# Attention as one row of tiles with values three tiles behind scores, batch preparation in fixed places, and a first MLP layer that starts before the output weights are prepared

## The chip, the cores and the metric

The kernel runs on one core of a Trainium2 chip. The metric is device time in microseconds (us) of one execution, lower is better. An engine is named as the profile names it: PE is TensorE's matmuls and PEld its weight loads, DVE is VectorE, ACT is ScalarE, POOL is GpSimd, and SP is SyncE, whose queue issues nearly every DMA.

## What is computed

Three stages in a chain. Attention over 4 batches, 8 heads, 576 rows of 64, in which only the scores within tau of their row's maximum count; then a gated MLP over the 2304 rows (called the first MLP here); then a mixture of 8 experts whose weights P come from a Sinkhorn iteration. Cut to what matters:

```python
scores = matmul(q, k.T) / sqrt(64)
scores = where(scores >= max(scores) - tau, scores, -1e9)
x = softmax(scores) @ v                      # 2304 x 512, heads side by side
xn = x / rms(x) * rms_g
x = (silu(xn @ w_gate) * (xn @ w_val)) @ w_out       # 512 -> 1536 -> 512
P = sinkhorn(exp(x @ w_gate2), 8 iterations)         # 2304 x 8
out = sum_e P[:, e] * (relu(x @ w1[e]) @ w2[e])      # 512 -> 1024 -> 512
```

## The kernel before

Every matmul is made in float16 from operands that are split into a high and a low part (high*high, high*low, low*high); the split needs a scale, a copy on ACT for the high part and a subtraction for the low part.

**Attention.** A batch has four row groups of 128 rows and a remainder of 64. A tile (`att_tile`, L254) is one head of one row group, or two heads of a remainder: 128 to a batch's 32 plus 4, 144 in all. For each tile TensorE makes scores S from qT, qX and kT into one of two PSUM buffers (L262); DVE takes the row maximum (L271), ACT the exponential (L276), DVE applies the threshold and the sum (L278); ACT and POOL split the result into hl (L283 to L285); a DMA transpose on SP turns it into eT (L287); then, within the same call, TensorE multiplies eT with the values vs into pv (L299). `att_main` (L339) runs 8 tiles of a row group, divides by the sums, and `finish_x` (L309) normalizes the row group and transposes it into xnT, which has two buffers of two row groups each. `att_rem` (L356) does the same for a remainder.

**Preparation of a batch.** `load_batch` (L140) loads raw keys, queries and values into three buffers; `prep_kq` (L179) finds the scales (GpSimd takes a square root by pow, L160), splits the keys chunk by chunk and transposes both halves of the heads into kT (L211); `prep_v` (L218) splits all values at once into vs; `prep_q` (L238) does one row group of queries.

**The first MLP.** `prep_in` (L412) prepares 512 columns of the gate or value weights: four chunks are loaded as 64-bit words, converted to float32 (`to_f32`, L394: ACT L402, DVE L403, L405, L406), squared on POOL (L425), their norms are summed by a matmul (L426), then scaled on ACT (L434), copied to the high part (L435) and subtracted on POOL for the low part (L436). There are three such groups (`prep_group`, L441). `prep_out` (L453) does 12 chunks of the output weights: conversion, absolute maximum on DVE (L459), a scale product (L476), scaling on ACT (L478), split (L479, L480). `mlp_block` (L494) takes two row groups: 12 column slices of the first layer into gv (L501), each through ACT, two DVE steps and a split into tT (L509 to L516); then the second layer for either row group (L529) and the writing of x2d for the last stage.

**What sets the order.** The program is traced in Python order, and the scheduler of the language lays out a fixed instruction stream for every engine: an instruction goes out when its inputs are there by the scheduler's own time model, the lowest priority number first, which is the trace order unless `tc.high_priority()` lowers it. Buffers (`bufs`) limit how far work runs ahead. In the kernel before, the start is traced as keys and queries of batch 0, weight group 0, values of batch 0; the loop over row groups traces attention at high priority, and after the second row group weight groups 1 and 2 and the output weights, then an MLP block after every second row group:

```python
    for i, (b, c) in enumerate(tiles):
        if c == 0 and b > 0:
            state[b] = prep_batch(b, raws.pop(b))
        ...
            with tc.high_priority():
                att_main(i, b, c)
        ...
        if i == 1:
            prep_group(1)
            prep_group(2)
            prep_out()
        if i % 2 == 1 and i > 1:
            mlp_block(i // 2 - 1)
```

So the MLP block of a pair is traced one pair later. The last stage (from L605 on) starts as the attention buffers are given back.

Of the kernel before, what the change touches and what calls it, by code (L numbers as in the profile page):

```python
# [7 lines left out]
F32 = mybir.dt.float32  # L8
F16 = mybir.dt.float16
# [10 lines left out]
def kernel(  # L20
# [43 lines left out]
    def pow2_scale(mx, n, bits, name, least=2.0**-100):  # L64

        s = small([P, n], name + "_s")
        inv = small([P, n], name + "_i")
        V.tensor_scalar(
            inv.bitcast(I32), mx.bitcast(I32), 0x7F800000, None, ALU.bitwise_and
        )  # L70
        V.tensor_scalar(inv, inv, least, None, ALU.max)
# [7 lines left out]
    half = small([P, 1], "half")  # L79
    V.memset(half, 0.5)  # L80
# [59 lines left out]
    def load_batch(b, which="kqv"):  # L140
        raws = []
        for nm, src in (("k", k), ("q", q), ("v", v)):
            if nm not in which:
                continue
            t = pa.tile([P, H, NW, D], F32, tag="raw", name=f"raw_{nm}{b}", bufs=3)
            nc.sync.dma_start(
                out=t[:, :, 0:NCH, :].rearrange("p h c d -> p h (c d)"),
                in_=src[b, :, 0 : NCH * P, :].rearrange("h (p c) d -> p h (c d)", c=NCH),
            )
            for o in (0, 64):  # L150
                nc.sync.dma_start(
                    out=t[o : o + REM, :, NCH, :],
                    in_=src[b, :, NCH * P : S, :].rearrange("h p d -> p h d"),
                )
            raws.append(t)
        return raws
# [22 lines left out]
    def prep_kq(b, raws):  # L179
        kr, qr = raws  # L180
        st = {}
        s_k, i_k = norm_scale(all_max(row_norms(kr, "km"), "kmx"), 1, 10, f"k{b}")
        qm = small([P, NW], "qm", bufs=2)
        for c in range(NW):
# [12 lines left out]
        st.update(wt=wt, bt=bt, c2=c2, qr=qr, s_q=s_q)  # L197

        st["q0"] = prep_q(b, 0, st)
        kT = [  # L200
            pa.tile([P, H // 2, S], F16, tag="kT", name=f"kT{b}_{a}", bufs=3) for a in range(2)
        ]
        for c in range(NW):
            n = P if c < NCH else REM
            ks = pa.tile([P, H, 2, D], F16, tag="ks", name=f"ks{b}_{c}", bufs=2)
            A.activation(ks[:, :, 0, :], kr[:, :, c, :], AF.Copy, scale=s_k[:, 0:1])
            V.scalar_tensor_tensor(
                ks[:, :, 1, :], kr[:, :, c, :], s_k[:, 0:1], ks[:, :, 0, :], ALU.mult, ALU.subtract
            )
            for a in range(2):  # L210
# [4 lines left out]
        st["kT"] = kT  # L215
        return st

    def prep_v(b, st, vr):  # L218
        s_v, i_v = norm_scale(all_max(row_norms(vr, "vm"), "vmx"), 1, 14, f"v{b}")
        vs = pa.tile([P, 2, H, NW, D], F16, tag="vs", name=f"vs{b}")  # L220
        A.activation(vs[:, 0], vr, AF.Copy, scale=s_v[:, 0:1])
        V.scalar_tensor_tensor(
            vs[:, 1].rearrange("p h c d -> p (h c d)"),
            vr.rearrange("p h c d -> p (h c d)"),
# [5 lines left out]
        st["vs"] = vs  # L230
        st["i_v"] = i_v

    def prep_batch(b, raws):
        st = prep_kq(b, raws[0:2])
        prep_v(b, st, raws[2])
        return st

    def prep_q(b, c, st):  # L238
        qs = pa.tile([P, H, 2, D], F16, tag="ks", name=f"qs{b}_{c}", bufs=2)
        qr, s_q = st["qr"], st["s_q"]  # L240
# [9 lines left out]
        return qT, qX  # L250
# [3 lines left out]
    def att_tile(b, c, st, qT, qX, heads, pv, sums, slot):  # L254

        kT, vs = st["kT"], st["vs"]
        sp = psa.tile([P, 2, 512], F32, tag="S", name=f"S{b}_{c}_{heads[0]}", bufs=2)
        rows = P // len(heads)
        for qq, first in ((qT, True), (qX, False)):
            for i, h in enumerate(heads):  # L260
                for j in range(2):
                    T.matmul(  # L262
                        sp[i * rows : (i + 1) * rows, j, 0:HS],
                        lhsT=qq[:, h, 0:rows],
                        rhs=kT[2 * h // H][:, h % (H // 2), j * HS : (j + 1) * HS],
# [4 lines left out]
        mx = pa.tile([P, 1], F32, tag="mx", name=f"mx{b}_{c}_{heads[0]}", bufs=4)  # L270
        V.tensor_reduce(mx, sv, AX.XY, ALU.max)  # L271
        nt = pa.tile([P, 2], F32, tag="nt", name=f"nt{b}_{c}_{heads[0]}", bufs=4)
        A.activation(nt[:, 0:1], mx, AF.Copy, scale=st["wt"][:, c : c + 1])
        e = pa.tile([P, S], F32, tag="e", name=f"e{b}_{c}_{heads[0]}", bufs=3)
# [7 lines left out]
        hl = pa.tile([P, 2 * S], F16, tag="hl", name=f"hl{b}_{c}_{heads[0]}", bufs=3)  # L282
# [3 lines left out]
        eT = pa.tile([P, 2 * S // P, P], F16, tag="eT", name=f"eT{b}_{c}_{heads[0]}", bufs=3)  # L286
        nc.sync.dma_start_transpose(out=eT, in_=hl)  # L287
        for i, h in enumerate(heads):
            o = pv[i * rows : (i + 1) * rows, slot * D : (slot + 1) * D]
            cols = slice(i * rows, (i + 1) * rows)  # L290
            mm = []
            for cc in range(NCH):
                mm.append((eT[:, cc, cols], vs[:, 0, h, cc, :]))
                mm.append((eT[:, cc, cols], vs[:, 1, h, cc, :]))
# [590 lines left out]
```

## Time and profile before

| | |
|---|---|
| time, median of 3 runs | 2223.94 us (2221.84 to 2225.57) |
| the profiled execution's own time | 2225.15 us |
| its span in the profile | 2223.4 us |
| TensorE busy | 2035.1 us, 92% of the span |
| DVE, ACT, POOL busy | 67%, 39%, 25% of the span |

The span runs from the first to the last event in the profile; the execution's own time has a little around it. Busy times are summed over the span, though the stages have different limits: attention and the first MLP fill roughly the first 800 us, the experts the rest. In the rows below, a row of a table by stage gives the stretch, its length, the busy time of each engine with the number of its instructions, the granted share of TensorE's full clock, the busy share of the DMA engines and what they moved in GB/s. TensorE's matmuls are pipelined, so the mean duration of one is longer than the distance from one to the next.

### The profile page before, as it was taken

To read this page: it belongs to the slowest core of one execution; us is meant where nothing else is said; L and a number is where in the kernel's file an instruction comes from. 1 tells how busy PE (TensorE), PEld (TensorE's weight loads), DVE (VectorE), ACT (ScalarE), POOL (GpSimd) and SP (SyncE) were. 2 spreads that over 40 slices of the span, in tenths; PEclk is the share of its full clock that TensorE was granted. 3 is DMA by queue.
4 is the path that set the end of the run, shared out by engine and by line. 5 is a ranking of instruction groups with operands and counts; after the bars stand their busy time and mean duration, and the time that the engine had idled before them with its cause. 6 is when DMAs were issued, how large, how long until landed. Compare 5 with 4: busy or idle time off the path is not lost.

```text
span 2223.4 us, 35280 instructions
## 1 busy us (share of the span) xinstructions
PE 2035.1 (92%) x13872; PEld 1193.9 (54%) x13872; DVE 1496.0 (67%) x2993; ACT 866.5 (39%) x1738; POOL 549.3 (25%) x638
## 2 busy tenths in 40 slices
PE   1337988999899998999999999999999999999999
PEld 0126667666776754555555555555555555555554
DVE  6997667776774267865676766757667666676554
ACT  4778677776773334221221222212212212222211
POOL 4867556564663321000010000000000000000000
PEclk9958999999999999999999999999999999999999
DMA  8976787777776042010010100001001001000001
GB/s 227 223 182 112 139 149 146 152 147 123 125 128 145 17 105 74 5 37 20 20 39 20 38 20 20 20 19 39 19 20 39 19 20 39 3 36 1 1 24 62
DMA packets 321880, 154.10 MB, mean 69 GB/s; under 512 B 278961, under 2 KB 292401, under 8 KB 321713
## 3 DMA queue, kind: packets, MB, share of 16 engines
q1 hardware_dynamic: 321120, 151.82, 30.4%
q8 instruction: 108, 1.77, 0.3%
q14 instruction: 60, 0.48, 0.1%
q0 software_dynamic: 64, 0.00, 0.0%
q10 hardware_dynamic: 528, 0.02, 0.0%
HBM read 68.18 MB, written 12.98 MB: 36 GB/s over the span
## 4 chain that ended last, share of the span: by engine, by line
PE 67%; DMA 2%; DVE 2%; SPq 1%; issue 1%; ACT 1%; POOL 1%; ACTq 0%; DVEq 0%; POOLq 0%
PE y L810 33%; PE h L764 28%; PE gv L501 4%; PE x L529 2%; SPq L666 1%; DMA w2r<-in_moe_w_dram 1%; DMA eT<-hl 1%; PE S L262 0%; DVE w L618 0%; PE pv L299 0%; DMA x2T<-x2d 0%; DMA w1r<-in_moe_w_dram 0%; PE logits L708 0%; POOL tT L516 0%; DMA qT<-qs 0%
## 5 line engine op out<-in xcount | busy, mean ns | idle before, releaser
L764 PE MATMUL h<-x2T,w 128*128 128x384 f16 x4032 | 704.6, 327 | 7.0 <-DMA x2T<-x2d 3.7
L764 PEld LDWEIGHTS <-w 128*128 128x128 f16 x4032 | 394.6, 98 | 297.4 <-issue 11.8
L825 DVE SCALAR_TENSOR_TENSOR acc<-y,coef,acc 128x512 f32<-128x512 f32 x270 | 198.3, 747 | 281.7 <-PE y L810 281.6
L634 POOL TENSOR_TENSOR w1s<-w1r 128x512 f32<-128x512 f32 x16 | 20.3, 1270 | 1063.2 <-DMA w1r<-in_moe_w_dram 1048.3
L810 PE MATMUL y<-w,hD 128*128 128x512 f16 x864 | 220.0, 379 | 0.0
L810 PE MATMUL y<-w,hA 128*128 128x512 f16 x864 | 211.9, 381 | 1.0 <-DVE acc L825 0.8
L810 PE MATMUL y<-w,hC 128*128 128x512 f16 x864 | 211.2, 381 | 0.2 <-ACT acc L821 0.2
L810 PE MATMUL y<-w,hB 128*128 128x512 f16 x864 | 210.4, 380 | 0.0
L284 POOL TENSOR_TENSOR hl<-e,hl 128x512 f16<-128x512 f32 x144 | 173.1, 1202 | 135.8 <-issue 70.5
L752 ACT ACTIVATE hA<-u 128x384 f16<-128x384 f32 x96 | 50.1, 522 | 342.3 <-DVE u L780 322.0
L501 PE MATMUL gv<-xnT,wg 128*128 128x256 f16 x1296 | 167.0, 276 | 11.8 <-DVE u L511 5.9
L752 ACT ACTIVATE hB<-u 128x384 f16<-128x384 f32 x96 | 50.2, 523 | 312.8 <-DVE u L784 311.9
L501 PE MATMUL gv<-xnT,wv 128*128 128x256 f16 x1296 | 167.1, 275 | 0.0
L529 PE MATMUL x<-wo,tT 128*128 128x512 f16 x648 | 144.5, 379 | 0.0
L501 PEld LDWEIGHTS <-wg 128*128 128x128 f16 x1296 | 126.2, 99 | 32.0 <-issue 14.1
L810 PEld LDWEIGHTS <-hB 128*128 128x128 f16 x864 | 84.7, 98 | 102.6 <-issue 1.1
L278 DVE SCALAR_TENSOR_TENSOR e<-S,nt,e 128x576 f32<-128x576 f32 x144 | 116.8, 812 | 32.7 <-ACT e L276 31.5
L299 PE MATMUL pv<-vs,eT 128*128 128x64 f16 x1792 | 82.8, 200 | 59.0 <-DMA eT<-hl 56.2
L299 PEld LDWEIGHTS <-eT 128*128 128x128 f16 (+1 forms) x2240 | 86.2, 104 | 94.0 <-DMA eT<-hl 80.9
L810 PEld LDWEIGHTS <-hD 128*128 128x128 f16 x864 | 84.7, 98 | 95.7 <-issue 0.6
L501 PEld LDWEIGHTS <-wv 128*128 128x128 f16 x1296 | 126.4, 99 | 16.2 <-issue 0.2
L810 PEld LDWEIGHTS <-hC 128*128 128x128 f16 x864 | 84.9, 99 | 92.5 <-issue 1.4
(254 smaller groups left out, 2950.2 us busy)
## 6 DMA issues: line engine op xcount, KB each, us to landing
w1r<-in_moe_w_dram SPq DMA_DIRECT2D x16, 1024.0 KB, 5.0
w2r<-in_moe_w_dram SPq DMA_DIRECT2D x16, 1024.0 KB, 5.5
wgatew<-in_moe_w_gate_dram SPq DMA_DIRECT2D x12, 512.0 KB, 4.8
wvalw<-in_moe_w_val_dram SPq DMA_DIRECT2D x12, 512.0 KB, 4.1
wo<-in_moe_w_out_dram SPq DMA_DIRECT2D x12, 512.0 KB, 4.1
x2d<-xs SPq DMA_DIRECT2D x24, 256.0 KB, 2.5
qX<-qT SPq DMA_DIRECT2D x40, 128.0 KB, 2.6
raw_k<-in_k_dram SPq DMA_DIRECT2D x4, 1024.0 KB, 6.0
```

The source lines that it names most:

```text
L278: V.scalar_tensor_tensor(ev, sv, nt[:, 1:2], ev, ALU.is_ge, ALU.mult, accum_out=sums[:, slot : slot + 1])
L284: G.tensor_tensor(hl[:, S + REM :], e[:, 0 : NCH * P], hl[:, 0 : NCH * P], ALU.subtract)
L299: T.matmul(o, lhsT=a, rhs=r, start=n == 0, stop=n == len(mm) - 1)
L501: T.matmul(gv[:, a, :], lhsT=w[:, l, kk, f * P : (f + 1) * P], rhs=xt[:, r * KD + kk, :], start=n == 0, stop=n == 3 * KD - 1,)
L529: T.matmul(ps, lhsT=tT[f][:, l, o : o + P], rhs=wo[:, f, r, :], start=n == 0, stop=n == 3 * KF - 1,)
L634: G.tensor_tensor(sm[:, 0], a21, a22, ALU.add)
L666: nc.sync.dma_start_transpose(out=xb[:, :, jj * P : (jj + 1) * P], in_=x2d[rows, :])
L752: A.activation(t[:, 0, :], src, AF.Relu)
L764: T.matmul(ps, lhsT=w[:, a, l, kk, f * P : (f + 1) * P], rhs=xb[:, b * 4 + r * 2 + kk, :], start=n == 0, stop=n == 5,)
L810: T.matmul(ps, lhsT=hs[a][f][:, l, jj * P : (jj + 1) * P], rhs=w2[:, r, f, :], start=n == 0, stop=n == 3 * KH - 1,)
L825: V.scalar_tensor_tensor(acc[i], ps, coef[h][:, i : i + 1], acc[i], ALU.mult, ALU.add)
```

## The change

A tile's value matmuls leave `att_tile` for `att_values`: the tile goes into a list `waiting`, and once more than three tiles wait, the first one's values are issued behind the last score matmul of the present tile (`tc.issue_after`). All tiles of all batches form one list, `row`. `prepare` puts each step of a batch's preparation at a fixed place of the row (o counts the 36 tiles of a batch): raw loads, scales, the two halves of keys (`prep_k`) and of values (`prep_v`), the queries. The row is traced with `attention_order`, which gives it priority numbers ahead of what was traced for the MLP; `first` moves on past the three weight groups, so these stay ahead of the later tiles, while the first layer of block 0, the output weights and its second layer come behind the tiles. `mlp_block` is cut into `mlp_in` and `mlp_out`, and for block 0 the output weights are prepared between the two. In the preparation of weights, square roots are taken by a shift of the exponent on DVE in place of pow on POOL, squares move from POOL to ACT, the low part from POOL to DVE with the scale folded into it (and ACT's scale pass goes), the scale of the output weights from ACT to DVE, and their maximum is replaced by a Square on ACT. The raw words of the output weights go through the buffers x2 and x2t.

The diff, cut to its core:

```diff
-    def pow2_scale(mx, n, bits, name, least=2.0**-100):
+    def pow2_scale(mx, n, bits, name, least=2.0**-100, root=False):
...
+        if root:
+            V.tensor_scalar(
+                inv.bitcast(I32), mx.bitcast(I32), 1, 0x7F800000,
+                ALU.logical_shift_right, ALU.bitwise_and,
+            )
+            V.tensor_scalar(inv, inv, 2.0**64, least, ALU.mult, ALU.max)
...
     def norm_scale(sq, n, bits, name):
-        G.tensor_tensor(sq, sq, half.to_broadcast([P, n]), ALU.pow)
-        return pow2_scale(sq, n, bits, name, 2.0**-60)
+        return pow2_scale(sq, n, bits, name, 2.0**-60, True)
...
+    def prep_k(st, a):
+        b, kr, s_k = st["b"], st["raw_k"], st["k"][0]
+        kT = pa.tile([P, H2, S], F16, tag="kT", name=f"kT{b}_{a}", bufs=3)
+        st["kT"].append(kT)
+        for c0 in range(0, NW, 2):
+            m = min(2, NW - c0)
+            ks = pa.tile([P, H, 2, D], F16, tag="ks", name=f"ks{b}_{c0}_{a}", bufs=2)
+            ks = ks.rearrange("p (c h) l d -> p c h l d", c=2)
+            for c in range(c0, c0 + m):
+                r, o = kr[:, a * H2 : (a + 1) * H2, c, :], c - c0
+                A.activation(ks[:, o, :, 0, :], r, AF.Copy, scale=s_k[:, 0:1])
+                V.scalar_tensor_tensor(
+                    ks[:, o, :, 1, :], r, s_k[:, 0:1], ks[:, o, :, 0, :], ALU.mult, ALU.subtract
+                )
+            for c in range(c0, c0 + m):
+                n = P if c < NCH else REM
                 nc.sync.dma_start_transpose(
-                    out=kT[a][:, :, c * P : c * P + n],
-                    in_=ks[0:n, a * H // 2 : (a + 1) * H // 2].rearrange("p h l d -> p (h l d)"),
+                    out=kT[:, :, c * P : c * P + n],
+                    in_=ks[0:n, c - c0].rearrange("p h l d -> p (h l d)"),
...
+    def prep_v(st, a):
+        b, s_v = st["b"], st["s_v"]
+        vs = pa.tile([P, 2, H2, NW, D], F16, tag="vs", name=f"vs{b}_{a}", bufs=2)
+        st["vs"].append(vs)
+        r = st["raw_v"][:, a * H2 : (a + 1) * H2]
+        A.activation(vs[:, 0], r, AF.Copy, scale=s_v[:, 0:1])
...
+    waiting = []
+    LAG = 3
...
+        waiting.append((st, heads, slot, group, eT))
+        if len(waiting) > LAG:
+            with tc.issue_after(last.ins):
+                att_values(*waiting.pop(0))
+    def att_values(st, heads, slot, group, eT):
+        if slot == 0:
+            group["pv"] = psa.tile([P, H * D], F32, tag="pv", name=f"pv{group['n']}", bufs=1)
+        rows = P // len(heads)
...
-            G.tensor_tensor(sq, raw[:, kk], raw[:, kk], ALU.mult)
+            A.activation(sq, raw[:, kk], AF.Square)
...
-        G.tensor_tensor(n2, n2, half, ALU.pow)
-        s, inv = pow2_scale(n2, 1, 9, f"{name}{gi}", 2.0**-60)
+        s, inv = norm_scale(n2, 1, 9, f"{name}{gi}")
         gs = small([P, KD], f"{name}gs{gi}")
         V.tensor_scalar(gs, g_sb, s[:, 0:1], None, ALU.mult)
         for kk in range(KD):
-            A.activation(raw[:, kk], raw[:, kk], AF.Copy, scale=gs[:, kk : kk + 1])
-            A.activation(w[:, 0, kk, cols], raw[:, kk], AF.Copy)
-            G.tensor_tensor(w[:, 1, kk, cols], raw[:, kk], w[:, 0, kk, cols], ALU.subtract)
+            sk, hi = gs[:, kk : kk + 1], w[:, 0, kk, cols]
+            A.activation(hi, raw[:, kk], AF.Copy, scale=sk)
+            V.scalar_tensor_tensor(w[:, 1, kk, cols], raw[:, kk], sk, hi, ALU.mult, ALU.subtract)
...
+            sq = to_f32(wo32[:, f], wd, f"wol{f}").bitcast(BF16)[:, 0:DM]
+            A.activation(sq, wo32[:, f], AF.Square, accum_out=om[:, f : f + 1])
...
-            A.activation(r, wo32[:, f], AF.Copy, scale=sf[:, 0:1])
+            r = rr[:, f % 2 * 2 : f % 2 * 2 + 2].rearrange("p o d -> p (o d)")
+            V.tensor_scalar(r, wo32[:, f], sf[:, f // n : f // n + 1], None, ALU.mult)
...
+    def attention_order():
+        return tc.high_priority(offset=tc.cur_priority - first)
...
+    SLOTS = len(row) // B
+    def prepare(b, o):
+        st = states[b]
+        if o < NCH * H and o % H == 1:
+            prep_q(st, o // H + 1)
+        if b > 0 and o in (LAG - 3, LAG - 1):
+            prep_v(st, (o - LAG + 3) // 2)
+        if b + 1 == B:
+            return
+        nx = states[b + 1]
+        early = b > 0
+        if o == (4 if early else 20):
+            nx["raw_k"] = load_raw("k", k, b + 1)
+            nx["raw_v"] = load_raw("v", v, b + 1)
+        if o == (10 if early else 23):
+            prep_k_scale(nx)
+        if o == (12 if early else 24):
+            prep_v_scale(nx)
+        if o == (18 if early else 26):
+            prep_k(nx, 0)
+        if o == 25:
+            nx["raw_q"] = load_raw("q", q, b + 1)
+        if o == 28:
+            prep_q_scales(nx)
+        if o == 32:
+            prep_q(nx, 0)
+        if o == 34:
+            prep_k(nx, 1)
...
+    for t in range(len(row) + LAG):
+        before = tc.cur_priority
+        with attention_order():
+            if t < len(row):
+                b, c, heads, n, g = row[t]
+                if n == 0:
+                    g["sums"] = pa.tile([P, H], F32, tag="sums", name=f"sums{g['n']}", bufs=2)
+                att_tile(states[b], c, heads, n, g)
+                prepare(b, t % SLOTS)
+            else:
+                att_values(*waiting.pop(0))
+            done = list(ended)
+            ended.clear()
+            for g in done:
+                (end_main if g["c"] < NCH else end_rem)(g)
+        first += tc.cur_priority - before
+        for g in done:
+            i = g["i"]
+            if i == 1:
+                for gi in range(NG):
+                    prep_group(gi)
+                first = tc.cur_priority
+                tT = mlp_in(0)
+                prep_out()
+                mlp_out(0, tT)
+            elif i is not None and i % 2 == 1 and i < len(tiles) - 1:
+                mlp_out(i // 2, mlp_in(i // 2))
```

## Rows read from the trace of the kernel before

**Rows 1.** Table by stage, all engines: busy us (x instructions), granted clock, DMA.

```profile
12.00:182.00 170.00, 54.17 (x386) 27.90 (x387) 161.50 (x317) 119.89 (x240) 119.07 (x108) 0.79 0.80 199
75.00:182.00 107.00, 40.77 (x353) 24.05 (x353) 104.48 (x205) 76.36 (x159) 80.19 (x76) 0.66 0.76 176
182.00:256.00 74.00, 68.75 (x739) 51.54 (x739) 48.03 (x108) 54.78 (x122) 41.97 (x55) 0.98 0.77 129
256.00:667.00 411.00, 374.06 (x4141) 285.26 (x4141) 287.22 (x682) 307.02 (x701) 259.45 (x349) 0.99 0.75 139
```

**Rows 2.** Waits of PE, 0 to 182 us: total us, times, longest.

```profile
PE pv L299 <- DMA eT<-hl: 32.4, 13, 4.8
PE S L262 <- DVE e L278: 29.3, 9, 6.9
```

**Rows 3.** Waits of PE, 182 to 667 us, same columns.

```profile
PE pv L299 <- DMA eT<-hl: 23.8, 29, 3.1
PE gv L501 <- DVE u L511: 5.9, 5, 2.2
PE pvr L299 <- DMA eT<-hl: 4.5, 4, 1.8
```

**Rows 4.** DMA issues: queue, count, median us to landing.

```profile
eT<-hl SPq DMA_TRANSPOSE x144, 3.4
```

**Rows 5.** Timeline of PE, six pieces: start us, us, instruction, count, idle before.

```profile
182.17 2.72 PE L501 MATMUL gv<-xnT,wg 128*128 128x256 f16 x12 [3.52 <-DMA xnT<-xn]
...
640.24 0.57 PE L299 MATMUL pv<-vs,eT 128*128 128x64 f16 x14
...
641.14 0.57 PE L299 MATMUL pv<-vs,eT 128*128 128x64 f16 x14
...
644.66 1.47 PE L501 MATMUL gv<-xnT,wg 128*128 128x256 f16 x12
...
645.97 1.04 PE L501 MATMUL gv<-xnT,wv 128*128 128x256 f16 x8
...
677.38 15.70 PE L529 MATMUL x<-wo,tT 128*128 128x512 f16 x72
```

**Rows 6.** Lines 0 to 182 us, by form: busy us, mean ns, idle before.

```profile
L262 PE MATMUL S<-kT,qT 128*128 128x288 f16 x46 | 15.2, 428 | 42.8 <-DVE e L278 29.3 <-DMA kT<-ks 10.8 <-DVE wval_i L68 2.3
...
L299 PE MATMUL pv<-vs,eT 128*128 128x64 f16 x266 | 17.1, 236 | 34.0 <-DMA eT<-hl 32.4 <-DVE vs L222 1.5
...
L459 DVE TENSOR_REDUCE om<-wo 128x1 f32<-128x512 f32 x12 | 8.1, 672 | 0.0
```

**Rows 7.** Stage 0 to 182 us of lines 403, 405, 406, 436: busy us.

```profile
0.00:182.00 182.00, 25.38 (x36) 0.80 0.80 200
...
0.00:182.00 182.00, 36.51 (x36) 0.80 0.80 200
...
0.00:182.00 182.00, 30.43 (x36) 0.80 0.80 200
...
0.00:182.00 182.00, 35.19 (x24) 0.80 0.80 200
```

**Rows 8.** Lines 403 and 405, 0 to 182 us: ns min/median/max, first and last start.

```profile
L403 DVE TENSOR_SCALAR wgatel<-wgatew x12: 410/446/1374, 16.0 to 87.0; 128x512 int32<-128x512 int32 x12
...
L405 DVE SCALAR_TENSOR_TENSOR wgatel<-wo,wgatel x12: 678/688/1637, 17.4 to 90.2; 128x512 int32<-128x512 int32 x12
```

**Rows 9.** Lines over the whole span: busy us, mean ns, idle before.

```profile
L278 DVE SCALAR_TENSOR_TENSOR e<-S,nt,e 128x576 f32<-128x576 f32 x144 | 116.8, 812 | 32.7 <-ACT e L276 31.5 <-POOL wo L480 0.6
...
L271 DVE TENSOR_REDUCE mx<-S 128x1 f32<-128x576 f32 x144 | 106.7, 751 | 36.6 <-PE S L262 36.1
...
L510 DVE SCALAR_TENSOR_TENSOR u<-u,gv 128x256 f32<-128x256 f32 x108 | 44.9, 417 | 85.3 <-ACT u L509 84.6
...
L222 DVE SCALAR_TENSOR_TENSOR vs<-raw_v,v_s,vs 128x2560 f16<-128x2560 f32 x4 | 12.8, 3202 | 2.2 <-ACT vs L221 2.2
```

**Rows 10.** Stage 95 to 182 us, PE's matmuls of tile S alone.

```profile
95.00:182.00 87.00, 18.46 (x68) 0.59 0.75 168
```

More of the change, by code (lines that the diff above doesn't have):

```diff
@@ L137, with load_raw @@
     psa = psa_cm.__enter__()
[L140 to L145, printed above, removed]
+    H2 = H // 2
+    def load_raw(nm, src, b):
+        t = pa.tile([P, H, NW, D], F32, tag="raw", name=f"raw_{nm}{b}", bufs=3)
+        nc.sync.dma_start(
+            out=t[:, :, 0:NCH, :].rearrange("p h c d -> p h (c d)"),
+            in_=src[b, :, 0 : NCH * P, :].rearrange("h (p c) d -> p h (c d)", c=NCH),
+        )
+        for o in (0, 64):
             nc.sync.dma_start(
-                out=t[:, :, 0:NCH, :].rearrange("p h c d -> p h (c d)"),
-                in_=src[b, :, 0 : NCH * P, :].rearrange("h (p c) d -> p h (c d)", c=NCH),
-            )
[L150 to L156, printed above, removed]
+                out=t[o : o + REM, :, NCH, :],
+                in_=src[b, :, NCH * P : S, :].rearrange("h p d -> p h d"),
+            )
+        return t
     def norm_scale(sq, n, bits, name):
-        G.tensor_tensor(sq, sq, half.to_broadcast([P, n]), ALU.pow)
-        return pow2_scale(sq, n, bits, name, 2.0**-60)
+        return pow2_scale(sq, n, bits, name, 2.0**-60, True)
     def row_norms(r, name):
@@ L196, in prep_kq @@
         V.tensor_scalar(wt, i_q, i_k[:, 0:1], nz8[:, 0:1], ALU.mult, ALU.mult)
[L197 to L210, printed above, removed]
+        st.update(wt=wt, bt=bt, c2=c2, s_q=s_q)
@@ L354, in att_main, with end_rem @@
         finish_x(i, x, st["i_v"][:, 0:1])
-    def att_rem(b):
-        st = state[b]
-        qT, qX = prep_q(b, NCH, st)
-        pv = psa.tile([P, H * D], F32, tag="pv", name=f"pvr{b}", bufs=1)
-        sums = pa.tile([P, H], F32, tag="sums", name=f"sumsr{b}", bufs=2)
-        for i in range(H // 2):
-            att_tile(b, NCH, st, qT, qX, [2 * i, 2 * i + 1], pv, sums, i)
-        rs = recip_sums(sums[:, 0 : H // 2], H // 2, f"rsumr{b}")
+    def end_rem(group):
+        i, st, pv = group["i"], group["st"], group["pv"]
+        b = st["b"]
+        rs = recip_sums(group["sums"][:, 0:H2], H2, f"rsumr{b}")
         if b % 2 == 0:
@@ L543, in mlp_block @@
             if pool is None:
-                x = pw.tile([P, 2, HD], F32, tag=f"x2{a}", name=f"x2f{i}")
+                if a == 0:
+                    x4 = pw.tile([P, 4, HD], F32, tag="x2", name=f"x2f{j}")
+                x = x4[:, 2 * a : 2 * a + 2]
             else:
@@ L551, in mlp_block @@
         if pool is None:
-            tt = pw.tile([P, 3, HD], F32, tag="x2t", name=f"x2t{j}")
+            tt = pw.tile([P, 4, HD], F32, tag="x2t", name=f"x2t{j}")
         else:
@@ new lines @@
+    first = tc.cur_priority
+    def attention_order():
+        return tc.high_priority(offset=tc.cur_priority - first)
+    row = []
+    for b in range(B):
+        for c in range(NW):
+            if c < NCH:
+                heads = [[h] for h in range(H)]
+            else:
+                heads = [[2 * h, 2 * h + 1] for h in range(H2)]
+            i = tiles.index((b, c)) if c < NCH else tiles.index((b, None)) if b % 2 else None
+            g = dict(st=states[b], c=c, i=i, n=f"{b}_{c}", last=len(heads) - 1)
+            row += [(b, c, hd, n, g) for n, hd in enumerate(heads)]
```

197 lines of the change are left out of this document (93 added, 104 removed).

## The prediction

> **What bounds the kernel now.** I read the table by stage first [rows 1]. From 12 to 182 us VectorE is busy 161.5 of 170 us (104.5 of 107 from 75 us on), while TensorE works in snatches, most of them at the lower of its two clocks (0.66 of full speed granted from 75 us on). From 182 us TensorE leads: 68.8 of 74, then 374 of 411 us. So the start is VectorE's and the rest TensorE's, and the time to win is TensorE's idle time.
>
> What it waits for is the second view [rows 2, 3]. Before 182 us: the transposed weights eT (32.4 us, in front of value matmuls) and the threshold step on VectorE that frees the score buffers (29.3). From 182 to 667 us eT again: 23.8 and 4.5 of (74 - 68.8) + (411 - 374) = 42 us. TensorE takes its instructions in order, so 14 value matmuls whose eT is 3.4 us in the DMA [rows 4] hold up the scores and MLP matmuls behind them.
>
> The timeline gives dates and prices [rows 5]. The first matmul of the first MLP starts at 182.2 us. At full clock 12 gate matmuls take 1.31 us from start to start, so a block's first layer costs 24 x 1.31 = 31.4 us; its second layer takes 15.7; and from one tile's values to the next tile's, with four score matmuls between, it is 0.90 us, the price of a tile.
>
> **TensorE's idle time at the start, before.** By 182 us it has done 46/2 = 23 tiles of scores and 266/14 = 19 of values [rows 6], 19 us, and 24 norm matmuls of 512 columns like the second layer's 15.7/72 = 0.22 us, 5 us. So 158 us are lost, and 74 - 68.8 = 5 more by 256 us, when block 0 is through both layers: 163.
>
> **The change at the start.** It lets the first layer begin as soon as two rows are there, and it reorders, adds to and lightens VectorE's work. That work is what has to be added up, since VectorE was full. By 182 us it has done 22 tiles and all weight chunks in 161.5 us [rows 1].
> - Gone: the 12 maxima of the output weights, 8.1 us [rows 6]. The Squares that replace them and GpSimd's squares go to ScalarE, where as many scale passes leave: no change, it is busy 120 of 170 us [rows 1].
> - New: 24 subtractions from GpSimd (35.2 us there) [rows 7]. Nearest are the other 512-wide instructions with two SBUF inputs, 0.68 us at best and 36.5/36 = 1.01 on average [rows 7, 8]; I take 0.9, as GpSimd gets emptier: 21.6 us (16 to 25). The output weights' scale, 12 times, comes over from ScalarE: as a 512-wide tensor_scalar 0.41 to 0.7, taken as 0.5: 6. The pow steps go from GpSimd to a shift in an instruction that was there: nothing.
> - Cheaper: the conversions of the 36 chunks. They took 25.4 + 36.5 + 30.4 = 92.3 us [rows 7]; at their minima of 0.41, 0.68 and, taken as its like, 0.68 [rows 8] they would take 63.7. These 28.6 us are lost beside GpSimd, busy 119 of 170 us [rows 1]. It loses the 35.2 us and 24 squares of the same shape, say 70 us, so six tenths come back: 17 (0 to 28.6).
> - Newly wanted by the same date: block 0's 24 elementwise steps of 0.417 us (10) [rows 9], a third of block 1's (3.3; four tT buffers let four of its twelve slices in before the second layer frees more), and the next batch's keys and values, which now rank ahead of the MLP (values 3.2 us [rows 9], the keys' ten smaller pieces about 6: 9; that halves double the instruction count costs 0.1 us a piece and is in it).
> Sum: 161.5 - 8.1 + 21.6 + 6 - 17 + 22.3 = 186 us, and 0.812 + 0.751 = 1.6 us for each tile past 22 [rows 9].
>
> How many tiles run before the output weights are ready no row shows. Tiles now outrank that preparation, up to a cap: xnT has two buffers, so the row stops when block 2 (to tile 52) wants a third, at about 54. The least is 24, with block 1 half done. Nearest is the rate of now: from 95 to 182 us 68/4 = 17 score tiles [rows 10], 5.1 us each; from some 50 us on that makes 30 to 33, and I take 30. Then VectorE needs 199 us: 57 by 75 us, as now, the other 142 at 0.976, date 75 + 145 = 220 us. TensorE has by then 30 x 0.9 + 31.4 + 10.5 + 5 = 74 us of work behind it and 146 idle: **17 us won** of 163. With 24 tiles: 211 us, 69 of work, 142 idle, 21 won. With 54: 260, 96, 164, nothing. The first gate matmul moves much further, to about 100 us (scores from 30 us, 16 tiles of 3 to 4 us, some 10 us to xnT); most of that lead is spent waiting for VectorE.
>
> Queues: SP keeps its 144 transposes for eT, its loads and the keys' transposes, at other dates. A raw load for the next batch stands in the row, and would hold up the eT transposes behind it if it had to wait for its buffer; it is asked for after the buffer's last reader, so I cost it at nothing. What covers it is the lag of three tiles; without that each batch would stall for part of a load.
>
> **From there to 667 us.** With values three tiles behind, eT has about three tiles' time, 12 us, for a 3.4 us transfer, so of the 28.3 us of waits 24 go; 4 stay where a group ends and the one pv buffer has to be read out. Late next is the chain of the scores (two buffers, freed by the threshold step). Bounds: 28 (nothing late next) and 5 (nearly all renamed). What follows attention changes no instruction: 0.
>
> **Sum.** The profiled execution took 2225.15 us (span 2223.4), 1.2 above the median of the runs, 2223.94. 2225.15 - 17 - 24 = 2184; against the median 2183.
>
> At one place the Trainium skill bears on the ledger. The rows show one conversion at 0.41 or at 1.37 us, the two-input one at 0.68 or 1.64 [rows 8]. GPSIMD Engine Reference, section Key points, says that GpSimd shares its SBUF interfaces with VectorE, and that they collide in VectorE's two-port mode and in instructions with two SBUF inputs. The spread agrees. The moved subtraction has two SBUF inputs, which speaks against moving it; emptying GpSimd speaks for it. By the rule alone all of the 28.6 us could come back instead of 17, as in the first rival.
>
> **Rivals.**
> - *Weights first, no collisions (faster, 2152).* Tiles only fill gaps, so 24 stand at the date (21 won), conversions run at their minima (11.6 us of VectorE, 12 won), all 28 us for eT go, and 10 of the other 14 us of waits from 182 to 667 us: 71 us. For it: VectorE is the only full engine and its conversions are stretched. Against: tiles outrank weights, and GpSimd keeps its part of every tile.
> - *The wait changes its name (2204).* ScalarE has 307 us of work in the 411 [rows 1]; packed into less, and in bursts whenever xnT comes free, its MLP steps come late, and TensorE waits for those in place of eT: 5 of 28 won, 15 at the start. Against: today TensorE waits for such steps 5.9 us [rows 3].
> - *The output weights starve (slower, 2244).* Their preparation ranks below every tile that the cap allows. With 54 tiles ahead, no relief in the conversions (+17) and the subtractions at 1.01 (+3), VectorE needs 186 + 51 + 20 = 257 us, the date is 280, and 96 us of work leave 184 idle, 21 lost; a stretch that tight leaves 5 of the eT gain at best, and loads that wait in the row cost a few us more: 19 lost. It comes out slower once the date passes 96 + 163 + 5 = 264 us, or 283 with the eT gain whole.
> That the change would not do what it says is hardly a rival: the lag is written into TensorE's queue.
>
> **How the numbers follow.** 0.46 for the forecast, 0.27 for weights first, 0.13 for the renamed wait, 0.14 for starving. About 4.5 us (0.2%) is what a measurement can tell from no change. Faster: 0.45 + 0.27 + 0.10 = 0.82; same: 0.01 + 0.02 + 0.02 = 0.05; slower: 0.01 + 0.12 = 0.13. The range runs from 2130, weights first with the bounds of its tile count and of the moved instructions, to 2222, which leaves out most of the starving case.
>
> **What would show it.** In the changed kernel's table by stage VectorE is 95% busy until about 220 us; the first gate matmul comes near 100 us, the second layer near 220, with about 30 tiles before it; waits of values for eT after that are under 6 us; conversions lie between their minima and today's means. It would be wrong if VectorE had holes before 200 us, the second layer came before 190 or after 260 us, or a new wait of over 15 us stood in the middle stretch.

## The result, and the profile after

The changed kernel took 2196.59 us (median of 4 runs, 2195.02 to 2199.54), the kernel before 2222.89 us beside it (4 runs, 2216.88 to 2225.57): a ratio of 0.989, 95% interval 0.9875 to 0.9904, so 1.1% or some 26 us faster. The forecast was 2183 in a range of 2130 to 2222: the sign and the range held, and of the 41 us forecast 26 came. The profiled execution took 2195.02 us (span 2193.2).

The table by stage of the changed kernel answers to [rows 1], with the same columns: stretch, length, busy time of TensorE, weight loads, VectorE, ScalarE and GpSimd, granted clock, DMA share and GB/s.

```profile
12.00:182.00 170.00, 75.55 (x634) 46.86 (x635) 154.40 (x340) 137.11 (x291) 57.68 (x64) 0.82 0.88 215
75.00:182.00 107.00, 58.45 (x587) 41.22 (x586) 98.53 (x208) 87.00 (x192) 49.87 (x56) 0.71 0.85 185
182.00:256.00 74.00, 61.08 (x637) 44.10 (x635) 59.08 (x143) 56.33 (x127) 45.12 (x53) 0.95 0.67 136
256.00:667.00 411.00, 386.91 (x4174) 292.50 (x4171) 286.93 (x679) 299.80 (x693) 246.41 (x337) 0.98 0.73 136
```

Read the TensorE column against [rows 1]. By 182 us it has been busy 21.4 us longer (75.55 against 54.17), from 182 to 256 us 7.7 less, from 256 to 667 us 12.9 more: 13.7 of the gain was there at 256 us, and 12.9 came later. GpSimd's time at the start has halved, from 119.07 to 57.68 us. VectorE is still nearly full (154.40 of 170).

The waits of TensorE, 0 to 182 us, answer to [rows 2]; those from 182 to 667 us, in the second fence, to [rows 3] (total us, times, longest).

```profile
PE pv L330 <- DMA eT<-hl: 27.6, 10, 4.7
PE wgaten L457 <- ACT wgateq L456: 24.5, 10, 9.4
PE S L282 <- DVE e L298: 19.1, 7, 6.9
```

```profile
PE pv L330 <- DMA eT<-hl: 19.6, 19, 3.8
PE S L282 <- DVE e L298: 5.2, 5, 1.9
PE S L282 <- DVE xm L571: 4.9, 1, 4.9
PE gv L530 <- DVE u L540: 2.7, 4, 1.5
PE pv L330 <- DVE xrem L395: 2.2, 1, 2.2
```

The surprise is the first line of the second fence: values still wait 19.6 us for eT, where [rows 3] had 23.8 and 4.5. A lag of three tiles was to have removed nearly all of it.

The conversions of the 36 weight chunks in 0 to 182 us (lines 433, 435 and 436, which are 403, 405 and 406 of [rows 7]), and in the fourth row the 24 subtractions that came over from GpSimd (line 466; the second figure, in us, is VectorE's):

```profile
0.00:182.00 182.00, 16.81 (x36) 0.83 0.88 215
...
0.00:182.00 182.00, 26.58 (x36) 0.83 0.88 215
...
0.00:182.00 182.00, 26.75 (x36) 0.83 0.88 215
...
0.00:182.00 182.00, 21.26 (x24) 0.83 0.88 215
```

The three steps take 70.1 us where they took 92.3, and the subtractions cost 21.3.

Two dates on the timeline of TensorE (compare [rows 5]: the first MLP matmul was at 182.17):

```profile
156.66 2.74 PE L530 MATMUL gv<-xnT,wg 128*128 128x256 f16 x12 [1.36 <-DMA xnT<-xn]
...
210.38 1.89 PE L561 MATMUL x<-wo,tT 128*128 128x512 f16 x8
```

The second layer of block 0 starts at 210.4 us (236.4 before). That date is a good yardstick: up to it TensorE has executed much the same in either kernel (954 matmuls in the changed one: scores of all 36 tiles of batch 0, the values of all but the last few, one first layer). The stretch from 12 us to that date, first of the kernel before, then of the changed one:

```profile
12.00:236.40 224.40, 104.09 (x1011) 70.01 (x1012) 199.68 (x405) 165.26 (x341) 157.41 (x158) 0.83 0.79 181
```

```profile
12.00:210.40 198.40, 101.64 (x954) 68.66 (x955) 182.40 (x410) 161.18 (x351) 79.51 (x88) 0.85 0.83 198
```

The date moved by 26 us: VectorE had 17.3 us less to do before it (199.68 to 182.40) and was idle 8.7 us less (24.7 to 16.0). Half of that was given back at once. From 220 to 240 us TensorE is busy only 13.3 us, because batch 1's scores and block 1's rows are not ready yet: in the second fence of waits, the 4.9 us are one wait of scores there. So a date that is 26 us earlier is worth 13.7 us of TensorE's time at 256 us.

### The profile page after: what moved, and what is told of

Its sections match the earlier page's. It is cut to its first block, busy times and chain, and to the rows that moved or that the text cites. A ratio compares the mean times of both kernels' runs of the same rounds, so it can differ in the third digit from the quotient of the medians.

```text
span 2193.2 us, 35334 instructions
## 1 busy us (share of the span) xinstructions
PE 2032.0 (93%) x13872; PEld 1194.7 (54%) x13872; DVE 1490.2 (68%) x3026; ACT 870.9 (40%) x1774; POOL 471.0 (21%) x572
## 4 chain that ended last, share of the span: by engine, by line
PE 70%; DVE 2%; DMA 1%; SPq 1%; POOL 0%; issue 0%; ACT 0%; DVEq 0%; ACTq 0%
PE y L906 33%; PE h L860 28%; PE gv L530 5%; PE x L561 2%; PE pv L330 1%; DMA w1r<-in_moe_w_dram 1%; SPq L762 0%; PE S L282 0%; DMA x2T<-x2d 0%; DVE w L714 0%; DMA w2r<-in_moe_w_dram 0%; DMA eT<-hl 0%; PE logits L804 0%; DVE w1m L725 0%; POOL xh L601 0%
## 5 line engine op out<-in xcount | busy, mean ns | idle before, releaser
L304 POOL TENSOR_TENSOR hl<-e,hl 128x512 f16<-128x512 f32 x144 | 172.8, 1200 | 228.2 <-ACT hl L303 146.2
L330 PE MATMUL pv<-vs,eT 128*128 128x64 f16 (+1 forms) x2240 | 103.1, 201 | 50.3 <-DMA eT<-hl 47.3
L330 PEld LDWEIGHTS <-eT 128*128 128x128 f16 (+1 forms) x2240 | 91.0, 106 | 79.1 <-DMA eT<-hl 62.1
```

The lines of the kernel that those rows point to most:

```text
L304: G.tensor_tensor(hl[:, S + REM :], e[:, 0 : NCH * P], hl[:, 0 : NCH * P], ALU.subtract)
L330: T.matmul(o, lhsT=a, rhs=r, start=n == 0, stop=n == len(mm) - 1)
```

## The experiments

Any edit makes the kernel's planner (the scheduler of the language) lay out every queue anew, and two small edits (the scale on ScalarE, the late loads below) came out 2 to 4 us off the changed kernel without a clear cause. With intervals of 0.0009 to 0.0017 on either side, a difference of under some 5 us between two variants is not read as an effect here. "Lost" below is the ratio less 0.989, times 2222.

| kernel | ratio to before (95%) | median us | lost us | second layer at | TensorE busy 12 to 256 | idle 256 to 667 |
|---|---|---|---|---|---|---|
| before | 1 | 2222.9 | 24 | 236.4 | 122.9 | 36.9 |
| changed | 0.9890 (0.9875 to 0.9904) | 2196.6 | 0 | 210.4 | 136.6 | 24.1 |
| VectorE step doubled | 1.0023 (1.0014 to 1.0032) | 2226.9 | 30 | 233.8 | 120.6 | 35.0 |
| GpSimd loaded | 1.0039 (1.0025 to 1.0054) | 2230.8 | 33 | 228.2 | 125.1 | 37.9 |
| two conversion steps | 0.9868 (0.9854 to 0.9882) | 2191.9 | -5 | 205.1 | 145.2 | 26.0 |
| and output squares on VectorE | 0.9905 (0.9888 to 0.9922) | 2199.2 | 3 | 198.6 | 148.5 | 30.6 |
| old division of weights | 0.9997 (0.9988 to 1.0006) | 2221.1 | 24 | 226.4 | 124.1 | 32.2 |
| before with new division | 0.9972 (0.9961 to 0.9982) | 2215.6 | 18 | 225.7 | 131.2 | 37.2 |
| output weights first | 0.9907 (0.9894 to 0.9921) | 2202.2 | 4 | 217.5 | 135.0 | 28.4 |
| scale on ScalarE | 0.9907 (0.9891 to 0.9923) | 2200.2 | 4 | 214.4 | 137.2 | 25.8 |
| planner's own lag | 0.9925 (0.9912 to 0.9939) | 2205.9 | 8 | 210.2 | 138.0 | 32.0 |
| lag of four | 0.9885 (0.9872 to 0.9898) | 2196.5 | -1 | 217.9 | 137.1 | 25.6 |
| preparation at the end | 0.9935 (0.9921 to 0.9949) | 2207.1 | 10 | 213.7 | 136.5 | 33.6 |
| late loads | 0.9901 (0.9885 to 0.9916) | 2200.7 | 2 | 211.4 | 137.7 | 25.0 |

The last two columns come from the table by stage of each profile. In most rows, what is lost there against the changed kernel adds up to about what the run lost; the loaded GpSimd (25 of 33) and the output squares are the exceptions.

The two columns cut every kernel at the same dates. A kernel that is late as a whole shows only a part of that before 256 us, and the rest as idle time behind it. So a second measure is needed: how late a kernel is at equal work. Every kernel here runs the same 13872 matmuls. The changed one has started 250,000 columns (of moving data, summed over its matmuls) at 262 us; against that, and against the end of its profiled span, the others are late by (us, minus for early):

| kernel | at 250,000 columns | at the end |
|---|---|---|
| before | 15.7 | 30.2 |
| VectorE step doubled | 27.7 | 35.1 |
| GpSimd loaded | 26.6 | 35.8 |
| two conversion steps | -12.3 | -6.8 |
| and output squares | -14.0 | 3.7 |
| old division | 17.6 | 23.3 |
| planner's own lag | -1.4 | 11.0 |
| preparation at the end | 2.7 | 12.2 |

(One profiled execution each; the ends lie up to some 6 us from what the medians give.) Most of what the doubled step and the loaded GpSimd cost is there at the start, though the stage table splits it about in half; the last two lose nearly all of theirs behind it.

### Is the start VectorE's?

**VectorE step doubled.**

```diff
         V.scalar_tensor_tensor(
             di, word[:, :, 1], -(2**31), lw, ALU.bitwise_and, ALU.bitwise_or
         )
+        V.scalar_tensor_tensor(
+            di, word[:, :, 1], -(2**31), lw, ALU.bitwise_and, ALU.bitwise_or
+        )
```

> The changed kernel with the third conversion step of each of the 36 weight blocks done twice (it repeats itself without changing anything): 36 more operations on VectorE, 26.8 us by the durations of the changed kernel, all before the output weights are ready. Theory 'VectorE's queue sets the end of the start': the second layer goes from 210 to 233 us or later and the kernel to 2214 to 2224 us (18 to 27 us more). Rival 'the weights' transfers or ScalarE set it': 2205 us or less.

Measured: 2226.9 us, 30 lost (a little above the theory's 18 to 27), second layer at 233.8. The added steps took 29.0 us by its profile:

```profile
12.00:240.00 228.00, 28.99 (x36) 0.80 0.74 176
```

They are paid in full, so VectorE's queue sets the date; transfers and ScalarE did not hide any of it.

**GpSimd loaded.**

```diff
-            to_f32(raw[:, kk], wd, f"{name}l{gi}_{kk}")
+            lw = to_f32(raw[:, kk], wd, f"{name}l{gi}_{kk}").bitcast(BF16)[:, 0:DM]
+            for _ in range(2):
+                G.tensor_tensor(lw, raw[:, kk], raw[:, kk], ALU.mult)
```

> The changed kernel with 48 more products on GpSimd, two behind the conversion of each of the 24 gate and value blocks; nothing reads them, and nothing else changes. GpSimd's busy time in 12 to 182 us goes from 57.7 to about 110, as under the old division. Theory 'VectorE's operations grow where GpSimd works beside them, and VectorE sets the end of the start': the 36 conversions go from 70 back to about 90 us and the kernel to 2212 to 2224 us (0.8 to 1.3 times the growth). Rival 'the old division cost by its chain over GpSimd, not by collisions': 2193 to 2204 us.

Measured: 2230.8 us, 33 lost, more than either theory's range. Nothing on VectorE was added, yet its conversions take 87.2 us, as the stretch from 12 to 240 us of lines 433, 435 and 436 shows (in the fourth row GpSimd's 48 products, line 456):

```profile
12.00:240.00 228.00, 21.97 (x36) 0.84 0.77 177
...
12.00:240.00 228.00, 33.90 (x36) 0.84 0.77 177
...
12.00:240.00 228.00, 31.37 (x36) 0.84 0.77 177
...
12.00:240.00 228.00, 58.11 (x48) 0.84 0.77 177
```

Against 70.1 in the changed kernel that is 17 us for 58 us of GpSimd's work; the 24 subtractions grew by 2.5 more (23.7). Single durations show how, ns min/median/max; first the changed kernel, then this one with GpSimd's products under it:

```profile
L435 DVE SCALAR_TENSOR_TENSOR wgatel<-wo,wgatel x12: 673/680/1637, 20.5 to 95.0; 128x512 int32<-128x512 int32 x12
```

```profile
L435 DVE SCALAR_TENSOR_TENSOR wgatel<-wo,wgatel x12: 680/1214/1637, 20.5 to 126.9; 128x512 int32<-128x512 int32 x12
...
L456 POOL TENSOR_TENSOR wgatel<-wo x24: 1034/1156/2168, 22.3 to 133.2; 128x512 bf16<-128x512 f32 x24
```

The minimum and the maximum stand where they stood; the median went from 680 to 1214 ns. An instruction meets a GpSimd operation or it doesn't, and one that does takes up to 0.96 us more, nearly the length of such an operation (1.03 at least).

The Trainium skill, SBUF — State Buffer, section "SBUF: two separate sides", says that the port pair shared by VectorE and GpSimd is an exclusive lock held for a whole instruction, and that the other engine blocks until then. These rows agree.

That GpSimd's work at the start costs VectorE time, and VectorE's time costs the run, is shown. VectorE's own work up to the second layer grew by 21 us (203.37, from 182.40). The other 12 of the 33 us are not accounted for. The products also stand in GpSimd's queue among what it does for the tiles and the first MLP, and this run does not tell that from the collisions.

**Two conversion steps.**

```diff
-        V.tensor_scalar(lw, word[:, :, 0], 29, None, ALU.logical_shift_right)
         di = dst.bitcast(I32)
-        V.scalar_tensor_tensor(lw, di, 3, lw, ALU.logical_shift_left, ALU.bitwise_or)
+        V.tensor_scalar(lw, di, 3, 4, ALU.logical_shift_left, ALU.bitwise_or)
```

> The changed kernel with a conversion of two steps on VectorE in place of three: the shift and the merge of the low word are left out, so that the weights carry 21 bits and not 24. VectorE loses 36 operations, 43.4 us to some 17 us of two of the three, 26 us in all. Theory 'VectorE sets the end of the start, in both directions': second layer near 190 us, 2170 to 2180 us. Rival 'ScalarE (137 of 170 us) or the transfers take over as soon as VectorE is relieved': 2186 to 2197 us.

Measured: 2191.9 us, 5 less than the changed kernel by the point values, with intervals that overlap. It is the one variant that may beat both kernels. Its stretch from 12 us to its second layer:

```profile
12.00:205.10 193.10, 98.96 (x953) 66.93 (x953) 164.32 (x389) 165.79 (x363) 75.06 (x94) 0.89 0.85 206
```

VectorE does 18 us less than in the changed kernel, and the date moves 5; TensorE's busy time up to 256 us rises by 8.6. VectorE's idle time rose from 16 to 29 us, ScalarE is now the fuller of the two (165.8 us). So what VectorE gets on top is paid in full, and of what it is spared only a part comes back: the second theory held.

**And output squares on VectorE.** On top of two steps, to relieve ScalarE.

```diff
-            A.activation(sq, wo32[:, f], AF.Square, accum_out=om[:, f : f + 1])
+            V.scalar_tensor_tensor(
+                sq, wo32[:, f], 1.0, wo32[:, f], ALU.mult, ALU.mult, accum_out=om[:, f : f + 1]
+            )
```

> The kernel with two conversion steps (weights of 21 bits, no low word), and the 12 squares of the output weights, 8.6 us of ScalarE, taken by VectorE instead (about 9 us there). With two steps VectorE was down to 172.9 of 208 us and the gain only 5 us. Theory 'ScalarE (169.5 of 208 us) was the next limit of the start': second layer before 202 us in place of 205.1, 2183 to 2188 us. Rival 'no engine is the limit any more, but the chain of the tiles through all of them': 2189 to 2196 us.

Measured: 2199.2 us, outside both ranges. The date did what ScalarE's theory asked (198.6 us), and TensorE's busy time up to 256 us is the highest of all. That is not more work, though: 1367 matmuls where two steps alone have 1383 (the columns agree within 0.5%), at a clock of 0.87 for 0.90. The run is slower all the same: in the middle stretch TensorE idles 30.6 us, and the granted clock from 256 to 400 us is 0.94 (0.98 in the changed kernel, 0.95 with two steps alone).

```profile
256.00:400.00 144.00, 126.76 (x1339) 91.66 (x1340) 99.85 (x245) 110.78 (x252) 80.46 (x110) 0.94 0.81 151
```

The start was lost early in this stretch: from 286 to 340 us TensorE ran 439 matmuls at 0.84, where two steps alone ran 491 at 0.94. An earlier start is not kept by itself. What let it slip there stays open.

### Which part of the change earned it?

**Old division of weights**, in the changed kernel; the output weights' Squares on ScalarE stay.

```diff
-            A.activation(sq, raw[:, kk], AF.Square)
+            G.tensor_tensor(sq, raw[:, kk], raw[:, kk], ALU.mult)
...
-            A.activation(hi, raw[:, kk], AF.Copy, scale=sk)
-            V.scalar_tensor_tensor(w[:, 1, kk, cols], raw[:, kk], sk, hi, ALU.mult, ALU.subtract)
+            A.activation(raw[:, kk], raw[:, kk], AF.Copy, scale=sk)
+            A.activation(hi, raw[:, kk], AF.Copy)
+            G.tensor_tensor(w[:, 1, kk, cols], raw[:, kk], hi, ALU.subtract)
...
-            V.tensor_scalar(r, wo32[:, f], sf[:, f // n : f // n + 1], None, ALU.mult)
+            A.activation(r, wo32[:, f], AF.Copy, scale=sf[:, f // n : f // n + 1])
```

> The changed kernel with the old division of the weight preparation: squares and low halves of the gate and value weights back on GpSimd, a scale pass of ScalarE ahead of the copy, the scale of the output weights back on ScalarE. VectorE loses 24 subtractions (21.3 us) and 12 scales, GpSimd gets 48 operations. Theory 'lighter GpSimd at the start earned it' (17 us of conversions): 2208 to 2216 us, conversions back to about 92 us in the first 182 us. Rival 'order earned it': 2192 to 2200 us, the conversions' loss paid by the 21 us of subtractions that VectorE is spared.

Measured: 2221.1 us: with the old division the rest of the change gains nothing. The conversions took 91.4 us, to within a microsecond those of before (0 to 240 us, lines 433, 435, 436):

```profile
0.00:240.00 240.00, 26.36 (x36) 0.85 0.74 182
...
0.00:240.00 240.00, 31.40 (x36) 0.85 0.74 182
...
0.00:240.00 240.00, 33.67 (x36) 0.85 0.74 182
```

VectorE's own total up to the second layer is only 7 us above the changed kernel's (189.5 us), since it is spared the subtractions; the rest of the 16 us by which that date is later is idle time of VectorE (25 us for 16). So the division gains in two ways, by fewer collisions and by fewer holes.

**Before with new division.** The same three edits the other way round, in the kernel before, which keeps its maxima and its 12 small scale instructions on VectorE.

> The kernel before with nothing changed but the division of the weight preparation (squares on ScalarE, low halves and the output scale on VectorE, no scale pass on ScalarE). Theory 'lighter GpSimd at the start earned it': 2203 to 2212 us. Rival 'order earned it' (tiles in one row, batch preparation in fixed places, first layer ahead of the output weights): 2218 to 2228 us, as the kernel before.

Measured: 2215.6 us, 5 to 6 us faster than before: between the two theories. Conversions 69.5 us, second layer 10.7 us earlier, 8.3 us more TensorE work by 256 us; nothing in the middle stretch (37.2 us idle). So neither the division nor the order brings the 26 us alone: 6, nothing, and 24 to 26 together. The two runs do not cut the change cleanly, since the maxima and the small scales stay with the order in both.

**Output weights first.**

```diff
-                tT = mlp_in(0)
                 prep_out()
-                mlp_out(0, tT)
+                mlp_out(0, mlp_in(0))
```

> The changed kernel with the output weights prepared ahead of the first MLP layer of block 0 (one line moved). If the early first layer fills TensorE's idle time in the stretch bound by VectorE: 6 to 10 us slower than the changed kernel (2202 to 2207 us), first gate product after 180 us. If the stretch is bound by VectorE whatever the order: 2194 to 2199 us, with the second layer earlier than 210 us by what the first one is later.

Measured: 2202.2 us, 4 lost, at the edge of what can be told and at the foot of the first theory's range. The first MLP matmul did not move (158.4 us for 156.7), against the first theory: it waits for its rows, not for its place. The second layer came 7 us later, against the second.

**Scale on ScalarE.**

```diff
-            V.tensor_scalar(r, wo32[:, f], sf[:, f // n : f // n + 1], None, ALU.mult)
+            A.activation(r, wo32[:, f], AF.Copy, scale=sf[:, f // n : f // n + 1])
```

> The changed kernel with the 12 scales of the output weights (8.6 us on VectorE) back on ScalarE as in the kernel before. Theory 'VectorE's queue sets the end of the start': second layer 5 to 9 us earlier than 210, 2188 to 2192 us. Rival 'the last blocks of the output weights hang on their chain, not on VectorE's queue, and ScalarE is the longer one in it': 2196 to 2202 us.

Measured: 2200.2 us, within what can't be told from the changed kernel; second layer at 214.4, 4 us later although VectorE has less to do: as the second theory had it. Just ahead of the second layer ScalarE is then the full engine (20.00 of 20 us from 200 to 220).

### What is the lag worth?

**Planner's own lag.** The values stand where the planner puts them.

```diff
-        waiting.append((st, heads, slot, group, eT))
-        if len(waiting) > LAG:
-            with tc.issue_after(last.ins):
-                att_values(*waiting.pop(0))
+        att_values(st, heads, slot, group, eT)
...
+        if o in (34, 35):
+            prep_v(nx, o - 34)
```

> The changed kernel, but the value products of a tile stand where the program's own scheduler puts them; everything else of the change stays. In the instruction order of TensorE the kernel before already had 3 or 4 scores tiles ahead of most values (103 of 144; 1 to 7 in all), the changed kernel 3 or 4 for 132. Theory 'the lag was there already': within 4 us of the changed kernel, 2193 to 2201 us, waits for eT as before. Rival 'the fixed lag of three tiles earned the gain': at least 10 us of the 26 go, 2207 us or more, and TensorE's waits of values for eT rise by as much.

The values' preparation moves with it, to the last two tiles of the batch before. Measured: 2205.9 us, 8 lost, between the two theories. On TensorE's timeline the values of some 125 of 144 tiles come 3 or 4 scores tiles behind even here. The start is the same; the loss is in the middle, 32.0 us idle for 24.1, and the wait for eT from 182 to 667 us is 26.7 us for 19.6. An even lag, with the values' preparation beside it, is worth something, but a third of what the prediction put on it.

**Lag of four.**

```diff
-    LAG = 3
+    LAG = 4
```

> The changed kernel with the values at least four tiles behind the scores in place of three. Theory 'eT is late because the lead is short': the 19.6 us for which TensorE waits for eT between 182 and 667 us fall below 8, 2182 to 2192 us. Rival 'eT has three buffers, so a tile's transpose waits for the values three tiles back however far the scores lead': the wait stays at 15 us or more, 2194 to 2204 us.

Measured: 2196.5 us, no change. This run shows best what the wait for eT is worth in the middle stretch. Its waits from 182 to 667 us:

```profile
PE S L282 <- DVE e L298: 10.2, 5, 3.2
PE pv L330 <- DMA eT<-hl: 8.5, 13, 2.0
PE gv L530 <- DVE u L540: 8.4, 9, 1.8
PE gv L530 <- ACT x2f L581: 3.5, 2, 2.3
PE x L561 <- DVE u L540: 3.2, 1, 3.2
```

The first theory is nearly right about the wait (19.6 to 8.5 us, with under 8 expected; so three buffers of eT were not the cause) and wrong about the time. Waits for score buffers and for MLP steps took its place: 5.2 to 10.2, 2.7 to 8.4, and 3.5 and 3.2 that were not there or were smaller. A wait that is last to end is not the only one that is due.

**Preparation at the end** of a batch, in one place.

```diff
+        if o == 32:
+            for nm, src in (("k", k), ("q", q), ("v", v)):
+                nx["raw_" + nm] = load_raw(nm, src, b + 1)
+        if o == 35:
+            prep_k_scale(nx)
+            prep_q_scales(nx)
+            prep_q(nx, 0)
+            prep_k(nx, 0)
+            prep_k(nx, 1)
+            prep_v_scale(nx)
```

(and the places spread over the tiles go.)

> The changed kernel with the preparation of the next batch in one place at the end of a batch, as before (loads at tile 32, all scales, keys and the first query at tile 35), in place of spread over its tiles; the halves of the values stay. Theory 'fixed places fill the boundary between batches': TensorE's idle time within 30 us of the three boundaries grows by 2 to 4 us each, 2202 to 2212 us. Rival 'the lead of the scores covers a boundary however the preparation stands': 2193 to 2201 us.

Measured: 2207.1 us, 10 lost, in the first theory's range, and all of it in the middle: 136.5 us of work by 256, then 33.6 us idle for 24.1. But the theory's place for it is not borne out. Within 30 us of the first score matmuls of batches 1, 2 and 3, TensorE idles 8.9, 5.1 and 7.7 us, in the changed kernel 12.0, 2.8 and 4.7: only 2.2 us more in all. The scores' lead at the ends of batches swings again between 3 and 7 tiles (as before: 1 to 7).

**Late loads.**

```diff
-        if o == (4 if early else 20):
+        if o == (8 if early else 20):
```

> The changed kernel with the loads of the next batch's keys and values issued at tile 8 of a batch in place of tile 4 (two of the three boundaries between batches). At the first one the loads stand in SP's queue at 228.2 us ahead of the last transpose of keys and of a query transpose, and TensorE works 13.3 of 20 us. If that order costs the idle time: 3 to 6 us faster (2190 to 2194 us). If the row of tiles is held by ScalarE and VectorE at the boundary whatever SP does: 2194 to 2199 us.

Measured: 2200.7 us (2194.3 to 2204.4), no gain, and a little above both ranges. TensorE is busy 14.5 us from 220 to 240 us where it was 13.3: the load in SP's queue is not what empties that stretch.

## Why the prediction was right and where it was wrong

- **VectorE sets the start: right.** The doubled step is paid in full. VectorE was 92% busy from 12 to 220 us (190.9 of 208; "95%" was forecast).
- **The terms of its bill: the large ones right, the sum too high.** Conversions: 22 us came back for "17" (0 to 28.6). Subtractions: 21.3 for "21.6". Scales: 8.65 us for "6", not all of them due by the date. Missed: 12 small instructions for the output scale (4.8 us) became one, and the queries' and other small steps shrank too. The bill is 186 us for 22 tiles, so 208 for 36 (14 x 1.56 more), and the date by it some 230 us; VectorE did 182.4 by 210.4. Beside the small steps, what it counted too high is the conversions (5 us), block 1's third (3.3) and part of the next batch's keys and values, which were not due by then.
- **The date of the second layer:** "220" with 30 tiles; it was 210.4 with all 36 tiles of batch 0 in the queue ahead. That these are near each other is luck: more tiles and a smaller bill. **TensorE's gain at the start** was 13.7 us for "17". The sum had a third of block 1's first layer ready ahead of that date; block 1 starts it only at 242.7 us, and in between TensorE ran short of work.
- **The first gate matmul: wrong.** Forecast "about 100 us" from 16 tiles of 3 to 4 us; it stood at 156.7 us. The second half of its rows was sent off only at 152.7, since the tiles shared VectorE with the conversions. Nothing in the sum hung on it, and its place in the code turned out to matter little (output weights first).
- **The failed step: "of the 28.3 us of waits 24 go".** 8.7 went (28.3 to 19.6), and TensorE's idle time from 256 to 667 us fell by 12.9. The step took "values three tiles behind" for something new. The kernel before had the values of some 100 of its 144 tiles 3 or 4 scores tiles behind already, on TensorE's timeline; the source put them behind their own tile, and the planner had moved them. The change only made the lag even: 1 to 7 tiles became 3 or 4 for 132 of 144. And where a longer lag does remove the wait (lag of four), the idle time stays.
- **Why a lead of three tiles does not cover eT.** The step set "12 us, for a 3.4 us transfer". The transfer is only the last link. In the changed kernel, over the 118 tiles whose values run from 182 to 667 us, eT lands 12.5 us after the tile's last score matmul (median; over 14.4 in a quarter of them; 12.7 in the kernel before). The links' own medians are 4.2 us to the end of the threshold step on VectorE, 3.9 more until the transpose is issued, and 3.4 in the DMA. So the lead is only as long as the chain, and a tile with a slower chain still waits.
- **The rival "the wait changes its name" (2204)** came nearer than the forecast by the time: 7 us off, for 14. Its mechanism is only half borne out. In the changed kernel most of the wait kept its name (19.6 us). With a lag of four it does change its name, but to waits that end on VectorE (10.2, 8.4 and 3.2 us) more than on ScalarE (3.5), which the rival blamed.
- **What the middle gained** is in part the early start itself: the doubled step and the loaded GpSimd keep the order and the lag, and idle 35.0 and 37.9 us there, largely because they start late. The even lag (8 us lost without it) and the preparation in fixed places (10 lost without it; costed at nothing in the prediction) are needed too. How these two act is not shown; near the changes of batch, where it was expected, they save only 2 to 3 us of idle time. The parts do not add up: 24 for the division, 10, 8 and 4 are more than the whole.
- The starving case did not come: the output weights were ready in time.

Open: what 12 of the 33 us under a loaded GpSimd were; how the even lag and the fixed places save time; why the old division falls another 6 us behind after its late start; and why the earliest start of all was lost again.

## What to carry to other kernels

Before you price a change of order, read the order that the kernel already executes, engine by engine: the source may say "at once" where the planner has long said "three later". A wait's total is a ceiling on what removing it gives, and can be far above it: lengthen the lag or free the buffer once as an experiment, and look at whether the idle time falls, not the wait. Set a lead against the whole chain that it has to cover, not against its last link. Compare two kernels at equal work before you say in which stretch time was lost. Where VectorE is full, count GpSimd's work beside it as part of VectorE's bill.

## What the runs showed of the hardware

48 GpSimd products that nothing waits for (58 us) added 17 us to 108 conversion steps and 2.5 us to 24 subtractions on VectorE; single instructions took 0.68 or up to 1.64 us. And relief of the fullest engine need not pay as its load costs: 29 us more on VectorE cost 30, 18 us less gave 5, with ScalarE the fuller one then (165.8 of 193 us).
